# Fused attention and GEGLU on one core: the order of a DMA queue, merged key and query loads, and the end of the kernel

## The chip, the cores and the metric

One core of a Trainium2 chip. The metric is the device time of one execution in microseconds (us), the median of several runs. The program is written with a tile framework: the author gives instructions in program order, and a list scheduler orders each engine's stream by simulated times, unless an engine's order is set by hand.

## The reference

```python
x = A_x                                        # 1 x 2048 x 576, fp32
xn = layernorm(x)                              # no scale, no bias
q, k, v = split(xn @ wqkv)                     # 32 heads of 18
p = softmax(q @ k.T * 18 ** -0.5)
s = (p @ v) @ wo                               # 576 x 576
g = silu((gelu_tanh(xn @ w_gate) * (xn @ w_up)) @ w_down)   # 576 -> 4608 -> 576
out = x + s * g
```

## The kernel before

Everything is fp32 accurate: an operand is cut into a high part (fp32r) and a low part, and a product is three matmuls, high by high, low by high and high by low. The kernel has four stages.

**Prologue.** Layernorm, transposes, the projections. Queries and keys go as high and low parts to `qk` in DRAM, values to `vs`, the normalized x transposed to `xhs`, the cut `wo` to `wos`.

**Sections.** The feed-forward net is 144 sections (`section`): 4 blocks of 512 tokens by 36 tiles of 128 of the 4608 hidden units. A section has 27 pairs of 64-row matmuls (`gate_up`, L421: gate and up at once in the two halves of the array), with work of attention put between them (`spread` over `specials`, and `hooks` before the i-th pair). x of the block stands in six tiles `xd` (high and low, three parts of three 64-row chunks); each is loaded to the lower 64 partitions (`load_xd`, L140, 384 KB) and copied to the upper 64 by `copy_xd` (L146 ScalarE for high, L147 GpSimd for low). The tiles have one buffer, so a new block's parts are loaded in the block's last section, after the 9th, the 18th and the last pair. Weights: `load_gu` (L126, two transfers of 288 KB, two buffers), cut into `wh` and `wl` by `split` on GpSimd (L106, L108). After a section come the activation (`activate`), the sums and cuts for a Strassen-like down projection (`sums_a` L456 to L461, `cut_a` L449, L450 on GpSimd), and after every second section the down products (`downs`, L533, added into `M` by VectorE, L537). Their cut weights `T` (2 MB) are formed in the first pass (`FORMED`), stored (`store_t`, L509) and loaded later (`load_t`, L475).

**Attention inside the sections.** Sections 11 to 138 carry attention: 32 units (8 groups of 4 heads by 4 query blocks), each of 4 sections. A section n has 8 score pairs (L784, exponential on ScalarE L785) of its key chunk and 8 maximum pairs (L749, reduction on VectorE L750), which run 40 slots ahead, and then the products with the values (`values`, L801). Keys are chunks of 512 tokens in 7 buffers of `KA`; a head takes 64 rows of the array: 18 rows high, 18 low, 18 high again (L715 `load_k`, 12 transfers of 36 KB), queries high, high, low (L737), and two rows with the negated maxima, high and low, that are zero (L738, 20 KB of zeros) until the maxima are known. `max_neg` reduces, cuts and transposes the maxima and stores them (L761); `max_end` fetches them, 8 rows by 8 transfers (L772). The lead sections 0 to 10 (`FIRST`) carry only the first unit's maximum pairs.

**Scaling and end.** `load_scale` (L670 `on`, L671 `od`), `scale` (L678), `store_scale` (L687) divide by the sums. The last five sections (`ENDS`) have no attention; between them stand the 16 output tiles: `load_wo` (woh 1.4 MB, wol 1.3 MB), `load_xy` (L916), `split_o`, `gate` (tanh of y on ScalarE L922, then VectorE L923), `project_o` (L933).

All DMAs are issued from SyncE. TensorE runs in program order (`manual_schedule`), the other engines, SyncE among them, in the scheduler's; `tc.keep_in_program_order` holds one instruction behind the one written just before it on its engine.

Of the kernel before, what the change touches and what calls it, by code (L numbers as in the profile page):

```python
# [45 lines left out]
ZR = HR - MROW  # L46
# [31 lines left out]
def kernel(ctx: ExitStack, tc: tile.TileContext, x, wqkv, wo, w_gate, w_up, w_down, out):  # L78
# [15 lines left out]
    mxT = [dram.tile([P, 8 * QD], F32, name=f"mxT{i}") for i in range(2)]  # L94
    ys = dram.tile([S - TB, D], F32, name="ys")
    zeros = dram.tile([P, ZR * TB // P], F32, name="zeros")
# [47 lines left out]
    def copy_xd(x, keep=lambda i: i):  # L144

        keep(nc.scalar.activation(x[0][HR:P], f(x[0])[0:HR], AF.Copy))  # L146
        keep(nc.gpsimd.tensor_copy(x[1][HR:P], x[1][0:HR]))  # L147
# [12 lines left out]
    with tc.tile_pool(name="pro", bufs=1) as pro, tc.tile_pool(name="pps", bufs=1, space=PSUM) as pps:  # L160
# [96 lines left out]
        zz = pro.tile([P, ZR * TB // P], F32, name="zz")  # L257
        nc.gpsimd.memset(zz, 0.0)
        nc.sync.dma_start(zeros, zz)
# [304 lines left out]
    def section(specials=(), tag="f", slots=False):  # L564
# [29 lines left out]
        for p in spread(pairs, specials, 1 if slots else None, hooks):  # L594
            p()
        if nxt:
            split_gu(nxt, NG - 1)
# [96 lines left out]

    with tc.tile_pool(name="att", bufs=1, reuse_waits="tile") as att:
        VS = [att.tile([P, VC * VW + 32 - DH - 1], F32, name=f"VS{i}") for i in range(VB)]
        for i, kk in enumerate(KS):
            for r in range(2):
                (nc.vector, nc.gpsimd)[i % 2].memset(f(kk[r]), 1.0)
        for vv in VS:  # L700
            nc.vector.memset(vv[:, VC * VW:], 0.0)

        def load_k(n, keep=lambda i: i, rs=(0, 1)):
# [4 lines left out]
            cols = slice(c * TB, (c + 1) * TB)  # L708
            for r in rs:
                for a in range(2):  # L710
                    kk = f(KS[n % KB][r])[64 * a:64 * a + MROW, :]
                    h = QD * (u % NQ) + 2 * r + a
                    rows = slice(D + h * DH, D + (h + 1) * DH)
                    for n_, i in enumerate((0, 1, 0)):
                        keep(nc.sync.dma_start(kk[n_ * DH:(n_ + 1) * DH, :], qk[i, rows, cols]))  # L715
# [11 lines left out]
        def load_q(u, rs=(0, 1)):  # L727
            j, g = divmod(u, NQ)
            cols = slice(j * TB, (j + 1) * TB)
            for r in rs:  # L730
                t = QS[u, r] = att.tile([P, TB], F32R, name=f"q{r}", bufs=3)
                for a in range(2):
                    q = f(t)[64 * a:64 * a + MROW, :]
                    h = QD * g + 2 * r + a
                    rows = slice(h * DH, (h + 1) * DH)
                    for n, i in enumerate((0, 0, 1)):
                        nc.sync.dma_start(q[n * DH:(n + 1) * DH, :], qk[i, rows, cols])  # L737
                    nc.sync.dma_start(f(t)[64 * a + MROW:64 * a + HR, :], zeros.rearrange("p c -> (p c)").rearrange("(r t) -> r t", t=TB))  # L738
# [13 lines left out]
        def max_neg(u, keep=lambda i: i):  # L752
# [3 lines left out]
            m2 = att.tile([P, 2, 4 * QD], F32R, name="m2", bufs=2)  # L756
            nc.vector.tensor_copy(m2[:, 0], nm)
            nc.vector.tensor_tensor(m2[:, 1], nm, f(m2)[:, 0], op=ALU.subtract)
            mt = att.tile([P, 8 * QD], F32, name="mt", bufs=2)
            nc.vector.transpose(mt, f(m2).rearrange("p i c -> p (i c)"))  # L760
            nc.sync.dma_start(mxT[u % 2], mt)  # L761
            NM[u] = True

        def max_end(u):

            del NM[u]
            parts = mxT[u % 2].rearrange("(q c) s -> c q s", q=4)
            for a in range(QD):
                for i in range(2):
                    row = 64 * (a % 2) + MROW + i  # L770
                    c = 4 * (i * QD + a)
                    nc.sync.dma_start(f(QS[u, a // 2])[row:row + 1, :].rearrange("o (t q s) -> o t q s", q=4, s=32),  # L772
                                      parts[c:c + 4].rearrange("(o t) q s -> o t q s", o=1))
# [18 lines left out]
        def values(u, kt):  # L792
# [42 lines left out]
        for r in range(2):  # L835
            load_k(0, rs=(r,))
            load_q(0, (r,))
        slot, chunk = 0, 1
        for n, m in enumerate(FIRST):
            none = [lambda: None]  # L840
            lead = [lambda s=s: max_pair(*divmod(s, NS)) for s in range(slot, slot + m)]
            section((n == 2) * 5 * none + lead + (m > 0 and n != 2) * none, "ring" if n == 1 else "f")
            if 0 in NM:
                max_end(0)
            if slot + m >= NS > slot:
                max_neg(0, tc.keep_in_program_order)
            slot += m
            while n > 0 and chunk < KB and chunk * SLOTS <= slot + SLOTS:
                load_k(chunk, tc.keep_in_program_order)
# [7 lines left out]
        ended, scaled = None, 0  # L857
# [168 lines left out]
```

## Time and profile before

| | |
|---|---|
| median of 3 runs | 2645.11 us (2644.92 to 2646.5) |
| the profiled execution, own time | 2650.72 us |
| its span, first to last instruction | 2648.9 us |
| TensorE busy | 2568.8 us, 97% |
| VectorE, GpSimd, ScalarE busy | 2157.7, 1600.7, 1463.6 us |
| mean granted clock of TensorE | 0.988 of full |
| DMA | 445.08 MB, 168 GB/s over the span |

In the views, PE is TensorE, PEld its weight load, DVE VectorE, ACT ScalarE, POOL GpSimd, SPq the queue of SyncE. A row of a timeline gives start, length, engine, line, operation, output<-inputs, a count, and in brackets how long the engine had been idle and what ended that. The rows of SPq are DMA issues; a row's length includes the wait before issues that it merges.

### The profile page before, as it was taken

What the parts mean: (1) busy time and instruction counts of PE and PEld (TensorE: products, weight loads), DVE (VectorE), ACT (ScalarE), POOL (GpSimd) and SP (SyncE); (2) the same over time, 40 slices, a digit from 0 to 9 for tenths busy, and PEclk for the clock granted to TensorE, in tenths of its full rate; (3) what the DMA queues carried; (4) which work ended last, traced back from release to release, by engine and by line L of the source; (5) the groups of instructions that cost most, each with busy time, mean ns of one, the idle gap of its engine ahead of it and who ended that gap; (6) DMA issues with size and microseconds to landing.
All of it is one profiled execution on the core that took longest, in us unless ns stands there. A gap on an engine that the chain in (4) does not pass through costs nothing.

```text
span 2648.9 us, 53876 instructions
## 1 busy us (share of the span) xinstructions
PE 2568.8 (97%) x20548; PEld 1852.7 (70%) x20548; DVE 2157.7 (81%) x2462; ACT 1463.6 (55%) x1741; POOL 1600.7 (60%) x1619
## 2 busy tenths in 40 slices
PE   9999999999989999999989999999998999999978
PEld 8887766666656666666656667666665666667768
DVE  5326899989978998998868888989887898988468
ACT  3222266666657655556556565555555666665622
POOL 2127688778777856666556555656556565555632
PEclk9999999999989999999989999999999999999989
DMA  8875355555565555555565555555565555556583
GB/s 258 261 242 145 86 165 162 166 164 163 160 180 168 168 159 163 164 162 166 164 159 170 165 161 158 162 160 159 158 166 136 159 160 160 160 157 166 163 246 128
DMA packets 393217, 445.08 MB, mean 168 GB/s; under 512 B 116732, under 2 KB 296444, under 8 KB 384384
## 3 DMA queue, kind: packets, MB, share of 16 engines
q1 hardware_dynamic: 392960, 441.64, 57.6%
q8 instruction: 164, 2.69, 0.4%
q14 instruction: 93, 0.76, 0.1%
HBM read 346.22 MB, written 95.28 MB: 167 GB/s over the span
## 4 chain that ended last, share of the span: by engine, by line
PE 75%; POOL 11%; DMA 6%; DVE 4%; issue 2%; ACT 1%; SPq 1%; POOLq 0%; DVEq 0%; ACTq 0%
PE pg L421 18%; PE acc L801 12%; PE py L533 12%; PE pu L421 9%; PE pe L784 7%; PE pm L749 7%; PE po L181 7%; DMA rawd<-in_B_w_down_dram 3%; POOL al L450 2%; POOL wl L108 2%; DMA xd<-xhs 1%; PE py L520 1%; POOL wh L106 1%; POOL T L498 1%; PE po L933 1%
## 5 line engine op out<-in xcount | busy, mean ns | idle before, releaser
L750 DVE TENSOR_REDUCE mx<-pm 128x2 f32<-128x1024 f32 x1024 | 1219.9, 1225 | 208.3 <-PE pm L749 200.9
L785 ACT ACTIVATE pT<-pe 128x1024 f32<-128x1024 f32 x1024 | 1047.6, 1026 | 615.3 <-PE pe L784 577.0
L421 PE MATMUL pu<-xd,wh 64*128 64x512 f32 x2538 | 933.8, 399 | 14.5 <-POOL xd L147 11.0
L421 PE MATMUL pg<-xd,wh 64*128 64x512 f32 x2538 | 932.8, 399 | 13.0 <-DMA xd<-xhs 7.8
L421 PEld LDWEIGHTS pg<-xd,wh 64*128 64x128 f32 x2538 | 471.7, 186 | 129.4 <-issue 61.5
L106 POOL TENSOR_SCALAR wh<-raw 128x384 fp32r<-128x384 f32 x432 | 236.3, 549 | 516.3 <-DMA raw<-in_B_w_up_dram 256.4
L421 PEld LDWEIGHTS pu<-xd,wh 64*128 64x128 f32 x2538 | 471.6, 186 | 41.4 <-POOL xd L147 14.1
L421 PE MATMUL pg<-xd,wl 64*128 64x512 f32 x1269 | 499.8, 394 | 0.0
L421 PE MATMUL pu<-xd,wl 64*128 64x512 f32 x1269 | 499.1, 393 | 0.0
L801 PE MATMUL acc<-pT,VS 128*32 128x512 f32 x4096 | 466.4, 596 | 0.0
L108 POOL TENSOR_TENSOR wl<-raw,wh 128x384 fp32r<-128x384 f32 x432 | 444.4, 1031 | 31.7
L784 PE MATMUL pe<-q,KA 64*128 64x512 f32 x2048 | 420.4, 397 | 14.2 <-DVE mx L750 7.2
L749 PE MATMUL pm<-KA,q 64*128 64x512 f32 x2048 | 422.4, 395 | 3.2 <-ACT pT L785 2.8
L533 PE MATMUL py<-T,ah 128*128 128x288 f32 x1876 | 384.4, 300 | 20.8 <-DVE M L537 17.1
L537 DVE TENSOR_TENSOR M<-py,M 128x576 f32<-128x576 f32 x448 | 337.7, 757 | 30.0 <-PE py L533 16.7
L533 PEld LDWEIGHTS py<-T,ah 128*128 128x128 f32 x1876 | 300.6, 189 | 76.7 <-issue 54.0
L801 PEld LDWEIGHTS acc<-pT,VS 128*32 128x32 f32 x4096 | 120.1, 109 | 277.5 <-issue 231.3
L450 POOL TENSOR_TENSOR al<-h,ah 128x512 fp32r<-128x512 f32 (+1 forms) x139 | 286.5, 2061 | 34.0 <-ACT ah L447 23.7
L784 PEld LDWEIGHTS pe<-q,KA 64*128 64x128 f32 x2048 | 196.5, 185 | 133.6 <-DVE mx L750 39.8
L533 PE MATMUL py<-T,al 128*128 128x288 f32 x938 | 277.4, 296 | 0.6 <-POOL al L450 0.6
L421 PEld LDWEIGHTS pg<-xd,wl 64*128 64x128 f32 x1269 | 236.3, 186 | 31.7
L421 PEld LDWEIGHTS pu<-xd,wl 64*128 64x128 f32 x1269 | 236.3, 186 | 12.3
(152 smaller groups left out, 2906.9 us busy)
## 6 DMA issues: line engine op xcount, KB each, us to landing
T<-ts SPq DMA_DIRECT2D x49, 2016.0 KB
KA<-qk SPq DMA_DIRECT2D x1536, 36.0 KB
raw<-in_B_w_gate_dram SPq DMA_DIRECT2D x144, 288.0 KB
raw<-in_B_w_up_dram SPq DMA_DIRECT2D x144, 288.0 KB
ts<-T SPq DMA_DIRECT2D x18, 2016.0 KB
VS<-vs SPq DMA_DIRECT2D x128, 152.0 KB
qk<-t SPq DMA_DIRECT2D x72, 256.0 KB
q<-qk SPq DMA_DIRECT2D x384, 36.0 KB
```

What stands on the lines that cost most here:

```text
L106: first = nc.gpsimd.tensor_scalar(hi, raw, 1.0, 1.0, op0=ALU.mult, op1=ALU.mult)
L108: keep(nc.gpsimd.tensor_tensor(lo, raw, f(hi), op=ALU.subtract))
L181: nc.tensor.matmul(o, st, m, start=(i == 0), stop=(i == len(terms) - 1))
L421: nc.tensor.matmul(o, w[1 + wp][k][rr, c, :], xd[k][xp][rr, c, :], start=(i == 0), stop=(i == len(terms) - 1))
L450: keep(two.tensor_tensor(lo, raw, f(hi), op=ALU.subtract))
L533: nc.tensor.matmul(py[:, t, 0:DC], h[:, i, tt], T[:, w, k], start=n == 0, stop=n == 2)
L537: nc.vector.tensor_tensor(M[:, m], py[:, :, 0:DC], M[:, m], op=ALU.add)
L749: nc.tensor.matmul(pm[:, a], QS[u, r][rr, t * P:(t + 1) * P], KS[(u * NA + c) % KB][r][rr, :], start=True, stop=True)
L750: nc.vector.tensor_reduce(MX[u][:, 2 * r:2 * r + 2, t, c], pm, axis=AX.X, op=ALU.max)
L784: nc.tensor.matmul(pe[:, a], KS[(u * NA + c) % KB][r][rr, t * P:(t + 1) * P], QS[u, r][rr, :], start=True, stop=True)
L785: nc.scalar.activation(PT[u, kt][:, 2 * r:2 * r + 2, :], pe, AF.Exp, scale=SCALE)
L801: nc.tensor.matmul(ACC[u][32 * a:32 * a + 32, :], VS[(u * NA + c) % VB][:, v:v + 32], pt[:, a, :], start=first, stop=last, skip_group_chec ...
```

## The change

- Both halves (r = 0, 1) of keys and of queries come by one transfer: 6 for a key chunk, 6 + 2 for queries, whose three tiles `QT` are now fixed and zeroed once; only the two rows of the maxima are zeroed again.
- The maxima are laid out so that 4 transfers store them and 2 fetch them; the fetch is at pair 10 of the next section.
- From the attention stage on, SyncE issues in program order. Some loads and stores are written at other places: `load_k` behind its section, the store of the outputs behind the values, `store_scale` one section later.
- `copy_xd` of the second and third part goes in three pieces each.
- In the lead sections ScalarE cuts the high part of the weights; the last three specials of every second one stand behind its pairs.
- At the end x and y of the first tile are loaded ahead of `wo`, the first gate comes behind section 1 of the end and not behind section 0, and an output's store is issued one tile later.

The diff, cut:

```diff
-def spread(pairs, specials, first=None, hooks={}):
+def spread(pairs, specials, first=None, hooks={}, tail=0):
+    specials, ends = specials[:len(specials) - tail], specials[len(specials) - tail:]
...
-    return out
+    return out + list(ends)

-    mxT = [dram.tile([P, 8 * QD], F32, name=f"mxT{i}") for i in range(2)]
+    mxT = [dram.tile([8 * QD, P], F32, name=f"mxT{i}") for i in range(2)]

-    def copy_xd(x, keep=lambda i: i):
-        keep(nc.scalar.activation(x[0][HR:P], f(x[0])[0:HR], AF.Copy))
-        keep(nc.gpsimd.tensor_copy(x[1][HR:P], x[1][0:HR]))
+    def copy_xd(x, keep=lambda i: i, i=slice(None)):
+        keep(nc.scalar.activation(x[0][HR:P, i], f(x[0])[0:HR, i], AF.Copy))
+        keep(nc.gpsimd.tensor_copy(x[1][HR:P, i], x[1][0:HR, i]))

     # section
+        one = split_ap if n + 1 < ATT.start else split
...
-                split_gu(nxt, k)
+                split_gu(nxt, k, one)
...
-                FF["hooks"].setdefault(8 * k - 7, []).append(lambda k=k: copy_xd(xd[k], keep))
+                for i in range(XG):
+                    FF["hooks"].setdefault(8 * k - 7 + 3 * i, []).append(lambda k=k, i=i: copy_xd(xd[k], keep, i))

+    ctx.enter_context(tc.manual_schedule(engines={mybir.EngineType.SP}))
...
+        QT = [att.tile([P, 2, TB], F32R, name=f"QT{i}") for i in range(3)]
+        for t in QT:
+            nc.gpsimd.memset(f(t), 0.0)

-            for r in rs:
-                for a in range(2):
...
-                    for n_, i in enumerate((0, 1, 0)):
-                        keep(nc.sync.dma_start(kk[n_ * DH:(n_ + 1) * DH, :], qk[i, rows, cols]))
+            load_heads(KA[:, i:i + 2], D, u % NQ, c, (0, 1, 0))
+
+        def load_heads(t, row, g, c, parts):
+            rows = slice(row + QD * g * DH, row + QD * (g + 1) * DH)
+            for a in range(2):
+                for m, i in enumerate(parts):
+                    o = HR * a + m * DH
+                    nc.sync.dma_start(f(t)[o:o + DH], qk[i, rows, c * TB:(c + 1) * TB].rearrange("(r a d) t -> a d r t", r=2, a=2)[a])

+        def max_store(u):
+            for q in range(4):
+                qq = slice(32 * q, 32 * q + 32)
+                nc.sync.dma_start(mxT[u % 2][:, qq], NM[u][qq])

     # max_end
+            for a in range(2):
+                o = HR * a + MROW
+                nc.sync.dma_start(f(QT[u % 3])[o:o + 2].rearrange("i r t -> i (r t)"),
+                                  mxT[u % 2][16 * a:16 * a + 16].rearrange("(i x) q -> i (x q)", i=2))

     # values, reciprocals
-                nc.sync.dma_start(oT[g, :, cols], acc)
+                at(u * NA + NA - 1, 1, nc.sync.dma_start, oT[g, :, cols], acc)
...
-            nc.sync.dma_start(rt.rearrange("a (c s) -> a c s", s=QD * TB // P), den)
+            at((u + 1) * NA + 3, 0, nc.sync.dma_start, rt.rearrange("a (c s) -> a c s", s=QD * TB // P), den)

     # lead sections
-            section((n == 2) * 5 * none + lead + (m > 0 and n != 2) * none, "ring" if n == 1 else "f")
+            section((n == 2) * 5 * none + lead + (m > 0 and n != 2) * none, "ring" if n == 1 else "f",
+                    tail=3 * (m > 0 and n % G == 0))

     # attention sections
-            if n > 0:
-                load_k(n - 1 + KB)
             section([p for s in range(s0, s0 + SLOTS) for p in slot_pairs(s)], slots=True)
+            load_k(n + KB)
...
             load_v(n + 2)
+            tasks(n, 1)
+            if ended:
+                max_store(um - 1)
+                FF["hooks"].setdefault(10, []).append(lambda v=um - 1: max_end(v))
             downs()
...
-                at(n + 1, 2, store_scale, scaled)
+                at(n + 2, 0, store_scale, scaled)

     # end
-                nc.sync.dma_start(out[rows, :], xx)
+                outs.append((out[rows, :], xx))
...
+        load_xy(0, 0)
         load_wo()
-        load_xy(0, 0)
...
         for i in range(ENDS):
             section([], "ring" if i % 2 else "f")
+            if i == 1:
+                ready()
             downs()
             finish()
-            if i == 0:
-                ready()
```

More of the change, by code (lines that the diff above doesn't have):

```diff
@@ L45 @@
 RING = 3
-ZR = HR - MROW
 DC, TH = D // 2, TB // 2
@@ L562, in gates, with section @@
         FF["gates"] = []
-    def section(specials=(), tag="f", slots=False):
+    def section(specials=(), tag="f", slots=False, tail=0):
         n = FF["n"]
@@ L593, in section @@
                 hook(9 * k + 9, lambda k=k: xd.append(load_xd(b + 1, k)))
-        for p in spread(pairs, specials, 1 if slots else None, hooks):
+        for p in spread(pairs, specials, 1 if slots else None, hooks, tail):
             p()
         if nxt:
-            split_gu(nxt, NG - 1)
+            split_gu(nxt, NG - 1, one)
         FF["w"] = nxt
@@ L725, with load_q @@
         QS, MX, ACC, SUM, PT, NM, DEN = {}, {}, {}, {}, {}, {}, {}
-        def load_q(u, rs=(0, 1)):
+        def load_q(u):
             j, g = divmod(u, NQ)
[L729 to L738, printed above, removed]
+            t = QT[u % 3]
+            load_heads(t, 0, g, j, (0, 0, 1))
+            for a in range(2):
+                o = HR * a + MROW
+                nc.sync.dma_start(f(t)[o:o + 2].rearrange("i r t -> i (r t)"), zeros)
+            for r in range(2):
+                QS[u, r] = t[:, r]
         def max_pair(u, i):
@@ L755, in max_neg @@
             keep(nc.vector.tensor_reduce(nm, MX[u].rearrange("p a t c -> p (a t) c"), axis=AX.X, op=ALU.max, negate=True))
-            m2 = att.tile([P, 2, 4 * QD], F32R, name="m2", bufs=2)
-            nc.vector.tensor_copy(m2[:, 0], nm)
-            nc.vector.tensor_tensor(m2[:, 1], nm, f(m2)[:, 0], op=ALU.subtract)
+            m2 = att.tile([P, 2, 2, 2, 4], F32R, name="m2", bufs=2)
+            n2 = nm.rearrange("p (r a t) -> p a r t", r=2, a=2)
+            nc.vector.tensor_copy(m2[:, :, 0], n2)
+            nc.vector.tensor_tensor(m2[:, :, 1], n2, f(m2)[:, :, 0], op=ALU.subtract)
             mt = att.tile([P, 8 * QD], F32, name="mt", bufs=2)
-            nc.vector.transpose(mt, f(m2).rearrange("p i c -> p (i c)"))
-            nc.sync.dma_start(mxT[u % 2], mt)
-            NM[u] = True
+            nc.vector.transpose(mt, f(m2).rearrange("p a i r t -> p (a i r t)"))
+            NM[u] = mt
+        def max_store(u):
+            for q in range(4):
+                qq = slice(32 * q, 32 * q + 32)
+                nc.sync.dma_start(mxT[u % 2][:, qq], NM[u][qq])
         def max_end(u):
             del NM[u]
[L767 to L773, printed above, removed]
+            for a in range(2):
+                o = HR * a + MROW
+                nc.sync.dma_start(f(QT[u % 3])[o:o + 2].rearrange("i r t -> i (r t)"),
+                                  mxT[u % 2][16 * a:16 * a + 16].rearrange("(i x) q -> i (x q)", i=2))
         def score_pair(u, i):
@@ L856 @@
             finish()
-        ended, scaled = None, 0
+        scaled = 0
         for n in range(NU * NA):
```

48 lines of the change are left out of this document (22 added, 26 removed).

## The prediction

> **What bounds the kernel now.** I read the page first, then busy time by stretch, then the timelines of single engines in the stretches that lose time.
>
> ```profile
> span 2648.9 us, 53876 instructions
> ...
> PE 2568.8 (97%) x20548; PEld 1852.7 (70%) x20548; DVE 2157.7 (81%) x2462; ACT 1463.6 (55%) x1741; POOL 1600.7 (60%) x1619
> ```
>
> TensorE sets the time: outside 80 us it is busy. So a change pays only where TensorE waits, or where it runs at a lowered clock after a wait. The second view is busy time by stretch: stretch and its length, then PE, PEld, DVE, ACT and POOL busy with their instructions, granted clock, DMA share, GB/s.
>
> ```profile
> 1226.24:1259.48 33.24, 33.24 (x283) 23.07 (x286) 28.89 (x31) 20.31 (x24) 20.13 (x21) 1.00 0.59 170
> 1329.56:1343.32 13.76, 13.76 (x119) 8.94 (x119) 12.26 (x13) 9.83 (x11) 9.86 (x9) 1.00 0.59 144
> 742.06:768.48 26.42, 20.70 (x120) 12.57 (x119) 11.54 (x11) 14.85 (x15) 21.48 (x20) 0.74 0.70 157
> 1362.76:1390.73 27.97, 18.05 (x123) 11.03 (x119) 11.47 (x11) 14.75 (x15) 15.63 (x15) 0.76 0.78 167
> 1983.24:2008.18 24.94, 17.50 (x119) 10.23 (x119) 11.62 (x11) 14.27 (x15) 17.75 (x17) 0.93 0.59 127
> 2513.35:2541.70 28.35, 10.19 (x86) 8.22 (x85) 10.57 (x16) 4.98 (x7) 6.48 (x10) 0.79 0.99 281
> 2541.70:2546.88 5.18, 5.18 (x21) 5.18 (x22) 3.82 (x6) 0.00 (x0) 2.95 (x3) 0.50 0.82 187
> ...
> 235.50:335.00 99.50, 93.63 (x717) 78.44 (x719) 81.36 (x90) 29.18 (x42) 63.42 (x66) 0.97 0.43 114
> ```
>
> Row 1 is a pair of sections in the attention loop: 33.24 of 33.24 us, nothing to win. Row 2 is one section with its values: 13.76 us. Rows 3 to 5 are the same work right after a change of token block: 12.66, 14.21 and 11.18 us more. Call them B1, B2, B3. Row 6 holds a hole at the end, where the DMA engines are full (share 0.99, 281 GB/s). The last row, the lead sections, has 5.87 us idle. B1 to B3 and the end hole are therefore the prize.
>
> **The block changes.** A new block's x is six transfers xd (384 KB each), copied to the upper partitions by ScalarE (high parts) and GpSimd (low parts). SyncE's queue at B2, B3 and B1:
>
> ```profile
> 1349.11 0.33 SPq L475 DMA_DIRECT2D T<-ts  x1
> ...
> 1350.82 11.28 SPq L715 DMA_DIRECT2D KA<-qk  x12
> ...
> 1363.65 4.03 SPq L140 DMA_DIRECT2D xd<-xhs  x6
> ...
> 1369.62 0.76 PE L421 MATMUL pg<-xd,wh 64*128 64x512 f32 x1 [6.79 <-DMA xd<-xhs]
> ```
> ```profile
> 1969.52 0.57 SPq L475 DMA_DIRECT2D T<-ts  x1
> ...
> 1972.76 4.47 SPq L140 DMA_DIRECT2D xd<-xhs  x4
> ...
> 1979.32 2.12 SPq L140 DMA_DIRECT2D xd<-xhs  x2
> ```
> ```profile
> 733.47 0.35 SPq L509 DMA_DIRECT2D ts<-T  x1
> 733.87 4.82 SPq L140 DMA_DIRECT2D xd<-xhs  x4
> ...
> 739.44 1.24 SPq L140 DMA_DIRECT2D xd<-xhs  x2
> ```
>
> At B2 the xd loads sit behind twelve key loads that block the queue for 11.28 us. At B1 the 2 MB store of T goes out just ahead of them. At B3 they already leave where the changed program's text puts them: two each after the 9th and 18th of the 27 pairs, the last two at the section's end. So B3 is a picture of B2 after the change, and its other engines show what is late next:
>
> ```profile
> 1982.76 1.48 ACT L146 ACTIVATE xd<-xd 64x1536 fp32r<-64x1536 f32 x1 [0.86 <-DMA xd<-xhs]
> ```
> ```profile
> 1984.77 1.46 POOL L147 CAST xd<-xd 64x1536 fp32r<-64x1536 f32 x1 [2.24 <-DMA xd<-xhs]
> ...
> 1990.13 1.46 POOL L147 CAST xd<-xd 64x1536 fp32r<-64x1536 f32 x1 [2.21 <-DMA xd<-xhs]
> 1991.67 1.28 POOL L459 TENSOR_TENSOR h<-h,h 128x512 f32<-128x512 f32 x1
> ...
> 1998.72 1.46 POOL L147 CAST xd<-xd 64x1536 fp32r<-64x1536 f32 x1
> ```
> ```profile
> 2000.23 0.50 PE L421 MATMUL pu<-xd,wh 64*128 64x512 f32 x1 [3.57 <-POOL xd L147]
> ```
>
> With T's 2 MB ahead the first part lands 10 us after its issue, the next 2.0 us later. Then GpSimd does 7.05 us of sums and cuts (1991.67 to 1998.72) between the second copy and the third, and TensorE waits 3.57 us for the third. Loads that start sooner don't remove that; only the order on GpSimd does, and the list scheduler still sets it.
>
> B3: the loads move by nothing. In pieces, the first third of a copy is done after a third of 1.46, about 0.5 us: TensorE's third part starts 1.0 us sooner. Gain 1.0. B2: B3's picture, plus on and od (0.5 MB, just behind T, estimated 1.3 us at twice B3's rate of 2.0 us per 384 KB, as those two go to 128 partitions and xd to 64). B3 loses 11.18, minus 1.0 for pieces, plus 1.3: 11.5. Gain 14.2 - 11.5 = 2.7. B1: the T store now stands behind xd, keys and values in the program. Its section begins at 742.06 - 13.76 = 728.3, so xd goes at 731.7 (a third of 10.2 us later), with no large transfer ahead. B2's first part took 6 us from 1363.65 to 1369.62, so here 737.7, then one each 2.0 us: the second low part 743.7, the third 747.7. First third copied 744.2, needed 745.8. Pieces to 745.3, then the 7.05 us of sums to 752.3, third part 752.8, needed 749.2: 3.6 us late, with the ScalarE copy about 4. Gain 12.66 - 4 = 8.7. Bounds: if GpSimd takes the copies ahead of its sums at all three, some 7 us more at B2 and B3 and 3 at B1; if it takes the sums ahead of the second copy too, up to 4 less at B1. Block changes: 8.7 + 2.7 + 1.0 = 12.4 (8 to 29). ScalarE's nine pieces cost two more fixed starts per copy, on an engine with 45% free.
>
> **The end.** The rows of SyncE, VectorE and TensorE, and the wait:
>
> ```profile
> 2513.35 0.38 SPq L475 DMA_DIRECT2D T<-ts  x1
> ...
> 2522.40 0.38 SPq L899 DMA_DIRECT2D wol<-wos  x1
> ...
> 2524.00 0.43 SPq L916 DMA_DIRECT2D yy<-ys  x1
> ```
> ```profile
> PE py L533 <- DVE M L537: 16.3, 1, 16.3
> ...
> 2523.63 0.50 PE L533 MATMUL py<-T,ah 128*128 128x288 f32 x2 [1.91 <-DMA T<-ts]
> ...
> 2537.44 0.76 DVE L923 SCALAR_TENSOR_TENSOR th<-th,yy 128x576 f32<-128x576 f32 x1 [14.02 <-ACT th L922]
> ...
> 2548.15 0.30 PE L933 MATMUL po<-woh,oh 128*128 128x288 f32 x1
> ```
>
> VectorE's gate for the first output tile waits for yy, which went out behind all of wo, 1.4 MB of woh and 1.3 MB of wol; the additions into M queue behind the gate, their PSUM buffers stay full, and TensorE stands 16.3 us. After: x and yy go ahead of wo. T stays where it is, 2513.4, and its products begin about 2523.6 as now. Behind it are 0.6 MB of x and yy, so yy is there around 2524, the gate 1.5 us later; products end at 2523.6 + 5.8 + 1.5 = 2530.9. The output product needs woh and wol: 2.0 + 0.6 + 1.4 + 1.3 = 5.3 MB at 281 GB/s from 2514 end at 2533, about 2535 with 2 us to land. So 2548.15 becomes 2535: 13.2. A wait of 4 us is left before it. What it costs in clock is unknown: after the 16.3 us the clock stood at 0.50 for 5.18 us (row 7), which is 2.6 us of work; B3's 3.57 us left its stretch at 0.93. I take 1.2 of 0 to 2.6, so 12 (bounds 3 to 17: 3 if wo comes as late as now, 17 if nothing waits). [...] Outputs stored one group later cost nothing: four x buffers cover them, and without that cover SyncE would hold the next loads for one addition on GpSimd, 2 us.
>
> **Merged transfers and queue order in the loop.**
>
> ```profile
> 1568.91 9.13 SPq L715 DMA_DIRECT2D KA<-qk  x12
> 1578.14 0.68 SPq L126 DMA_DIRECT2D raw<-in_B_w_gate_dram  x1
> ...
> 2037.17 4.28 SPq L715 DMA_DIRECT2D KA<-qk  x12
> ```
> ```profile
> 1583.62 0.98 POOL L106 TENSOR_SCALAR wh<-raw 128x384 fp32r<-128x384 f32 x2 [9.96 <-DMA raw<-in_B_w_up_dram]
> ```
>
> Twelve key loads take 4.28 us to issue when free, six 2.1; queries go from 16 issues to 8, the maxima's rows from 1 + 8 to 4 + 2. All run beside a busy TensorE: worth 0 on the path. If the cover were gone, it would be 2.1 us a section. Order: raw weights now go at a section's top. At 1568.5 that is 9.6 us sooner than the 1578.14 shown; every other one waits for the values' end (the next at 1582.5, against 1586 now), since the V load waits there for TensorE, and T, outputs and raw queue behind it. Key chunk n+7 leaves at the end of section n and is read in section n+2, 13.76 us later. The store of the maxima waits for VectorE's transpose; behind it stand the raw loads, and who waits is GpSimd, two sections ahead of need. So 0, with rival 3 as the bound above. Three more memsets of queries fall on GpSimd before the first section.
>
> **The lead.**
>
> ```profile
> 188.56 0.66 SPq L126 DMA_DIRECT2D raw<-in_B_w_gate_dram  x1
> ```
> ```profile
> 189.65 4.27 DVE L699 MEMSET KA<- 128x512 f32 x8
> ```
> ```profile
> 204.98 0.39 PE L421 MATMUL pgu<-xd,wh 64*128 64x512 f32 x2
> ```
>
> The weights of section 1 went out at 188.56. In program order they stand behind 14 key and query loads, which wait for the memset at 189.65: 190.2 + 14 x 0.36 = 195.2, cut by about 202 (5.5 us lie between the issue at 1578.14 and the cut at 1583.62), needed at 204.98. No loss; if the query buffers come free only at 199, it is 5 to 8 us. Against that, ScalarE's share of the cuts can win at most the 5.87 us idle of the lead. Three maxima at the tail of five sections each set up to one reduction (1.2 us) ahead of the down products. I take 0 (-6 to +8).
>
> **Sum.** 12.4 + 12 = 24.4. The profiled span 2648.9 becomes 2624.5; the profiled run's own time, 2650.72, about 2626; the median, 2645.11, about 2620.5. A difference of 0.2% (5.3 us) is about what a measurement tells from none.
>
> **Rivals.**
> 1. The new queue order makes the scheduler put the copies ahead of GpSimd's sums. For it: smaller pieces leave openings. Against: in all three traces' stretches that I read, the sums came before the third copy. Gains 11.7 + 9.7 + 8 + 12 = 41: 2604.
> 2. The end hole only changes its cause, T and wo on full DMA engines instead of yy: for it, share 0.99; against, 16 us is more than 5.3 MB need. Gains 12.4 + 3: 2630.
> 3. Slower: in strict order the raw loads wait behind the V load and land too late for GpSimd's cuts, each pair of sections. The loop has 64 pairs; it decides from 24.4 / 64 = 0.38 us a pair. At 0.7 us it costs 45: 2665. For it: GpSimd already waits up to 9.96 us for raw. Against: the cut is then two sections ahead of use, and raw goes out earlier, not later.
> 4. It doesn't do what it says: the other engines are re-sorted around the same waits, a new VectorE gate stands in front of M, and nothing is left: 2643.
>
> **How the numbers follow.** Forecast 0.45, rival 1 0.25, rival 2 0.12, rival 3 0.12, rival 4 0.06. The range runs from 2598 (rival 1 with some lead gain) to 2642 (rival 2 with the lead's 8 us and B1's 4), and leaves out rival 3 and most of rival 4. Faster: 0.45 + 0.25 + 0.12 + 0.01; same: 0.05 of rival 4; slower: rival 3.
>
> **What would show it.** Right: the stretch after B1 is near 18 us, B2 25, B3 24; the six xd loads leave before any key load; TensorE's 16.3 us wait for M is gone and one of some 4 us for wol stands before the first output product; row 1's pair stays 33.2 us. Wrong: pairs of sections longer than 33.2 us, a TensorE wait for wh or KA in the loop, GpSimd's third copy ahead of its sums, or the first section 1 matmul later than 205.

## The result and the profile after

The changed kernel takes 2673.3 us (median of 4 runs, 2670.96 to 2675.37) against 2645.02 (2641.91 to 2646.5) before: ratio 1.0108, interval [1.0091, 1.0126]. It is slower by 28 us; 2620.5 was forecast. The page, first lines, and the stretches that answer to those of the prediction (start and end, length, then PE, PEld, DVE, ACT, POOL busy, granted clock, DMA share, GB/s): B1, B2, B3, the pair and the lead.

```profile
span 2670.2 us, 52622 instructions
...
PE 2573.9 (96%) x20548; PEld 1850.8 (69%) x20548; DVE 2146.0 (80%) x2462; ACT 1476.0 (55%) x1783; POOL 1585.5 (59%) x1604
```
```profile
762.44:779.60 17.16, 15.80 (x124) 9.26 (x121) 11.80 (x12) 14.28 (x19) 12.89 (x15) 1.00 0.91 259
1374.93:1406.62 31.69, 18.95 (x119) 11.81 (x120) 11.78 (x12) 15.45 (x19) 17.79 (x20) 0.73 0.57 119
1996.34:2018.74 22.40, 18.03 (x120) 11.28 (x120) 11.73 (x12) 15.56 (x19) 16.22 (x18) 0.85 0.67 145
1237.94:1271.12 33.18, 33.18 (x283) 23.15 (x279) 29.01 (x31) 20.30 (x24) 20.13 (x21) 1.00 0.60 168
243.88:350.03 106.15, 93.87 (x719) 77.93 (x715) 77.25 (x90) 37.24 (x60) 55.20 (x50) 0.95 0.34 85
```

B1 (17.16 us) and B3 (22.40) came out about as forecast (18, 24), the pair is unchanged, B2 (31.69, forecast 25) is worse than before, and the lead is 7 us longer. Where the time went is read best from TensorE's progress. All traces hold the same 20,548 matmuls, nearly in the same order, so the starts of number 1000, 2000, 2200, 5400, 5900, 10350, 10700, 15400, 15800, 19600 and 20000 cut each run into the same pieces of work, from the first matmul's start to the last one's. First column: us of before; then the difference to it for the changed kernel and for five of the experiments below.

| piece | before | change | e1 | e4 | e9 | e12 | e13 |
|---|---|---|---|---|---|---|---|
| prologue | 187.0 | -1.4 | -1.1 | +0.1 | -0.3 | -1.2 | -0.7 |
| lead | 136.7 | +10.4 | +3.1 | +3.2 | +1.6 | +4.8 | -1.1 |
| loop's start | 24.5 | +6.1 | -0.1 | -0.1 | -0.2 | -0.1 | 0.0 |
| first block | 387.2 | +5.4 | +7.5 | +5.6 | +5.0 | -1.7 | -1.3 |
| around B1 | 78.5 | -10.5 | -3.3 | -9.4 | -9.4 | -10.6 | -9.4 |
| second block | 536.1 | +2.2 | +1.5 | +2.0 | +2.5 | +0.7 | +1.2 |
| around B2 | 60.4 | +3.1 | +1.3 | +4.9 | -8.4 | -8.7 | -8.4 |
| third block | 565.3 | -2.1 | +0.1 | -0.6 | -1.6 | -1.4 | -0.9 |
| around B3 | 64.4 | -2.0 | +3.2 | -2.7 | -7.1 | -9.1 | -9.0 |
| fourth block | 455.0 | +1.0 | +2.1 | -0.1 | +0.3 | +2.9 | +0.2 |
| end, first part | 70.8 | -4.4 | +3.7 | -2.5 | -2.3 | -4.2 | -2.0 |
| end, second part | 73.8 | +13.4 | 0.0 | +2.4 | +0.7 | +1.8 | +1.9 |

The profiled run of before (2650.72 us) lies 5.7 above its median, and the changed kernel's (2671.98) 1.3 below its own, so the change's column sums to 21 where the medians differ by 28; the other columns are too low by some 4 to 8 in the same way. Single pieces of unchanged work wander by 1 to 3 us from run to run.

**The lead.** TensorE's waits in 200 to 350 us (total, times, longest), then SyncE's queue:

```profile
PE pgu L421 <- ACT wh L112: 6.1, 1, 6.1
PE pm L756 <- ACT pT L794: 5.1, 1, 5.1
PE py L520 <- DVE mx L757: 3.1, 5, 0.6
```
```profile
184.85 13.39 SPq L305 DMA_DIRECT2D vs<-vn  x8
198.34 2.12 SPq L724 DMA_DIRECT2D KA<-qk  x6
...
203.69 0.66 SPq L126 DMA_DIRECT2D raw<-in_B_w_gate_dram  x1
```

Section 1's weights leave at 203.69, not at 188.56: in program order they stand behind eight value stores, which wait up to 1.5 us each, 10.8 us together, for ScalarE to write their tiles. TensorE stops for 6.1 us and comes back at a granted clock of 0.53:

```profile
203.79:209.90 6.11, 0.00 (x0) 0.00 (x0) 1.98 (x3) 4.20 (x7) 1.26 (x1) 0.83 0.92 215
209.90:214.90 5.00, 4.71 (x22) 3.41 (x24) 0.00 (x0) 2.91 (x6) 4.78 (x5) 0.53 0.63 158
```

The second wait, 5.1 us, starts at SyncE too (its own waits, 290 to 340 us): the store of the first maxima waits 21 us for VectorE's transpose at the head of the queue, the next raw weights behind it leave at 324.43 instead of 305.57, GpSimd cuts and sums late (it waits 8.86 us for raw and begins at 331.64), and ScalarE's cut of T, which waits 7.77 us for the sums and begins at 337.52, stands ahead of the exponentials pT (339.50).

```profile
SPq L774 <- DVE mt L768: 21.0, 1, 21.0
```

Nothing leaves SyncE for those 21.0 us: the issue before them ends at 298.92, the next one begins at 319.99.

**The first block.** TensorE's waits for pT (total, times, longest), one every four sections, and SyncE, GpSimd and ScalarE around one of them:

```profile
PE pm L756 <- ACT pT L794: 5.0, 5, 1.8
```
```profile
456.05 1.71 SPq L774 DMA_DIRECT2D mxT<-mt  x4
457.85 0.37 SPq L509 DMA_DIRECT2D ts<-T  x1
458.32 0.60 SPq L126 DMA_DIRECT2D raw<-in_B_w_gate_dram  x1
```
```profile
469.93 0.51 POOL L106 TENSOR_SCALAR wh<-raw 128x384 fp32r<-128x384 f32 x1 [6.82 <-DMA raw<-in_B_w_up_dram]
```
```profile
475.94 1.17 ACT L490 ACTIVATE T<-tsum 128x1152 fp32r<-128x1152 f32 x1 [8.07 <-POOL tsum L483]
...
477.92 1.92 ACT L794 ACTIVATE pT<-pe 128x1024 f32<-128x1024 f32 x2
```

**B2.** SyncE, TensorE's waits, and GpSimd:

```profile
1361.24 0.33 SPq L475 DMA_DIRECT2D T<-ts  x1
1361.74 0.32 SPq L672 DMA_DIRECT2D on<-oT  x1
1362.11 0.56 SPq L673 DMA_DIRECT2D od<-rT  x1
1362.71 0.67 SPq L126 DMA_DIRECT2D raw<-in_B_w_gate_dram  x1
1363.43 3.63 SPq L126 DMA_DIRECT2D raw<-in_B_w_up_dram  x1
1367.16 8.64 SPq L140 DMA_DIRECT2D xd<-xhs  x6
```
```profile
PE pg L421 <- DMA xd<-xhs: 6.0, 1, 6.0
PE pu L421 <- POOL xd L147: 5.7, 1, 5.7
```
```profile
1375.32 1.26 POOL L680 TENSOR_TENSOR on<-on,od 128x512 f32<-128x512 f32 x1 [8.96 <-DMA od<-rT]
...
1379.96 1.26 POOL L459 TENSOR_TENSOR h<-h,h 128x512 f32<-128x512 f32 x1
...
1388.64 3.14 POOL L147 CAST xd<-xd 64x1536 fp32r<-64x1536 f32 x4
```

T, on, od and raw, 3.1 MB, go ahead of xd; its first part lands about 13.7 us after its issue (1367.16 to 1380.84, where ScalarE's copy begins). GpSimd, too, stands 8.96 us for od, which is behind T, so its sums and cuts start late and its copies of xd, the first one among them, come behind them at 1388.64.

**The end.** SyncE, VectorE, TensorE's waits from 2515 us on, and SyncE's own wait for stored outputs in the changed kernel (2550 to 2660 us) and, for the same stage, before (2535 to 2640 us):

```profile
2530.56 0.56 SPq L837 DMA_DIRECT2D rT<-rec  x1
2531.21 0.39 SPq L475 DMA_DIRECT2D T<-ts  x1
2532.33 0.34 SPq L925 DMA_DIRECT2D xx<-in_A_x_dram  x1
2532.73 0.59 SPq L925 DMA_DIRECT2D yy<-ys  x1
```
```profile
2542.91 0.76 DVE L932 SCALAR_TENSOR_TENSOR th<-th,yy 128x576 f32<-128x576 f32 x1 [6.52 <-ACT th L931]
...
2548.29 0.75 DVE L537 TENSOR_TENSOR M<-py,M 128x576 f32<-128x576 f32 x1
```
```profile
PE py L533 <- DVE M L537: 8.5, 5, 6.6
PE po L942 <- DVE ol L917: 7.7, 2, 5.7
```
```profile
SPq L925 <- DMA out_dram<-xx: 38.4, 11, 8.6
```
```profile
SPq L916 <- DMA out_dram<-xx: 7.5, 5, 2.1
```

In program order T goes behind the store of the last reciprocals, which waits 13.6 us for VectorE, and yy behind T. The gate still stands ahead of the additions into M. The second wait is new: an output product waits 5.7 us for a cut that stands on VectorE behind the next gate, whose yy came late. It came late because the load of x ahead of it on SyncE waits until an earlier output, in the same buffer, has landed in DRAM: 11 times, 38.4 us in all, against 7.5 us before.

### The profile page after: what moved, and what is told of

Same layout as the page of the kernel before. It is cut to its first block, busy times and chain, and to the rows that moved or that the text cites. A ratio compares the mean times of both kernels' runs of the same rounds, so it can differ in the third digit from the quotient of the medians.

```text
span 2670.2 us, 52622 instructions
## 1 busy us (share of the span) xinstructions
PE 2573.9 (96%) x20548; PEld 1850.8 (69%) x20548; DVE 2146.0 (80%) x2462; ACT 1476.0 (55%) x1783; POOL 1585.5 (59%) x1604
## 5 line engine op out<-in xcount | busy, mean ns | idle before, releaser
L106 POOL TENSOR_SCALAR wh<-raw 128x384 fp32r<-128x384 f32 x402 | 218.1, 547 | 448.2 <-DMA raw<-in_B_w_up_dram 234.3
L756 PE MATMUL pm<-KA,QT 64*128 64x512 f32 x2048 | 417.8, 396 | 16.3 <-ACT pT L794 15.4
L108 POOL TENSOR_TENSOR wl<-raw,wh 128x384 fp32r<-128x384 f32 x402 | 415.5, 1038 | 26.0
L793 PE MATMUL pe<-QT,KA 64*128 64x512 f32 x2048 | 418.3, 397 | 12.8 <-DVE mx L757 8.2
L793 PEld LDWEIGHTS pe<-QT,KA 64*128 64x128 f32 x2048 | 196.4, 185 | 130.1 <-DVE mx L757 29.3
L756 PEld LDWEIGHTS pm<-KA,QT 64*128 64x128 f32 x2048 | 202.5, 186 | 66.5 <-ACT pT L794 24.7
```

Of the source, the lines that this page charges most:

```text
L106: first = nc.gpsimd.tensor_scalar(hi, raw, 1.0, 1.0, op0=ALU.mult, op1=ALU.mult)
L108: keep(nc.gpsimd.tensor_tensor(lo, raw, f(hi), op=ALU.subtract))
L756: nc.tensor.matmul(pm[:, a], QS[u, r][rr, t * P:(t + 1) * P], KS[(u * NA + c) % KB][r][rr, :], start=True, stop=True)
L793: nc.tensor.matmul(pe[:, a], KS[(u * NA + c) % KB][r][rr, t * P:(t + 1) * P], QS[u, r][rr, :], start=True, stop=True)
```

## The experiments

All ran beside the kernel before. Theory S: the strict order on SyncE loses the time, where an issue that waits stands ahead of a load that TensorE needs soon. Rival R: the change's other parts lose it.

**e1: no strict order.**
```diff
-    ctx.enter_context(tc.manual_schedule(engines={mybir.EngineType.SP}))
```


> The changed kernel without the line that puts SyncE's issues in program order; all its other parts stay. Theory S (strict order on SyncE is what loses): the lead loses 15 us less (no 6.1 us wait for the first cut weights of section 1, no 5.1 us wait at the loop's start) and the end about 9 less, while the block changes may lose their 10 us of gain again, because the 2 MB store of T may stand ahead of xd again: 2640 to 2658 us, the first section 1 matmul near 205 us. Theory R (the other parts lose: ScalarE's share of the weight cuts, three maxima at the tail of a lead section, the first gate later): the time stays within 5 us of 2673.

2667.14 us (1.0082 [1.0066, 1.0098]): outside both forecasts. The table shows why the sum moves by only 6: the order costs 13.5 in the lead and loop's start and 13.4 in the end's second part, and it earns 7 at B1, 5 at B3 and 8 in the end's first part. The first block loses with and without it; without it TensorE's waits there are others (3.8 us for VectorE's sums `accs`, none for pT), so the other parts cost something there too.

**e2: that line alone, on the kernel before.**
```diff
+    ctx.enter_context(tc.manual_schedule(engines={mybir.EngineType.SP}))
     with tc.tile_pool(name="att", bufs=1, reuse_waits="tile") as att:
```


> The kernel before, with that one line alone added at the same place. Theory S: the lead's raw weights wait behind the value stores and the key and query loads, here 28 issues instead of 14, so the lead loses 15 us or more; with the end 2660 to 2680 us. Theory R: within 5 us of 2645.

2782.85 us (1.0518 [1.0502, 1.0533]), far over what S expected. The first block alone is 78 us longer, and its waits (340 to 830 us, TensorE's and SyncE's own) are those of the changed kernel tenfold:

```profile
PE pm L751 <- ACT pT L787: 48.7, 12, 4.8
```
```profile
SPq L724 <- PE acc L803: 80.9, 6, 14.5
SPq L763 <- DVE mt L762: 79.6, 6, 14.2
```

The value load and the maxima's store wait at the head of the queue and raw waits behind them. So what else the change does, the places that it gives them in the program above all, makes the order bearable; no run separates the places from the merged transfers.

**e3, e4: strict order from the attention loop on; and in the loop alone.**
```diff
         scaled = 0
+        strict = ExitStack()
+        strict.enter_context(tc.manual_schedule(engines={mybir.EngineType.SP}))
         for n in range(NU * NA):
...
+        strict.close()        # e4 only
```


> The changed kernel with the strict order beginning only at the attention loop, so that the lead sections are list-scheduled on SyncE. Theory S: the lead's 15 us come back and nothing else moves: 2658 (2655 to 2662). Theory R: the lead's loss stays, 2673.

> As the one before, and the strict order also ends after the attention loop, so that the end sections and the output products are list-scheduled on SyncE. Theory S: the lead's 15 us and the end's 9 come back, the block changes keep their 10 and the end may gain some of what was forecast: 2635 to 2649. Theory R: 2673.

2664.57 (1.0069 [1.0052, 1.0086]) and 2652.31 (1.0020 [1.0008, 1.0032]). Both lie above what S expected (2655 to 2662, 2635 to 2649). The difference between them, 12.3 us, is nearly all the end's second part (+13.6 and +2.4): S holds there. In the lead and the loop's start the order is worth 7.2 + 6.2 us; some 3 stay.

**e5: the changed kernel, two issues moved in the lead.**
```diff
+                if b == NB - 1 and j in (0, 1):      # among the value stores
+                    early[j + 1] = load_gu(j + 1, tc.keep_in_program_order)
...
-                max_store(0)
+                FF["hooks"].setdefault(3, []).append(lambda: max_store(0))
```


> The changed kernel, strict order and all, with two issues moved in the program: the raw weights of sections 1 and 2 among the value stores of the last token block, and the store of the first maxima to the fourth pair of the next section, behind that section's raw loads. Theory S (what waits at the head of SyncE's queue is what loses, in the lead the value stores and the maxima's store): the waits of 6.1 us (203.8) and 5.1 us (335.5) go, the lead is some 7 and the loop's start 6 us shorter: 2658 to 2662 us. Rival R (ScalarE's cuts and the maxima at a section's tail lose the lead): less than 3 us of change, 2670 to 2675.

2667.31 (1.0095 [1.0079, 1.0111]), between the two forecasts. The 6.1 us wait is gone, and the loop's start waits 2.1 us instead of 5.1, as S says. The lead gives back only 2 of its 10: new waits for `wl` (3.4 us in all) come in, as GpSimd has the same cuts to do.

**e6: the changed kernel, T ahead of the store of the last reciprocals.**
```diff
             downs()
-            tasks(n, 2)
+            if n < NU * NA - 1:
+                tasks(n, 2)
             finish()
+            if n == NU * NA - 1:
+                tasks(n, 2)
```


> The changed kernel with the last T load ahead of the store of the last reciprocals in program order, nothing else. Theory S: T goes out when its buffer is free (about 2525 instead of 2531), the 8.4 us of wait at 2539 to 2549 shrink to some 3: 5 us less at the end's first part, 2667 to 2669; the waits for yy at 2586 stay. Rival (DMA engines full at the end, the cause only changes): the hole keeps its length, 2672 to 2674.

2676.57 (1.0125 [1.0110, 1.0140]), above both forecasts: S's step failed, and the hole changed its cause, as the rival says. T left at 2526.4 and its wait went. But xx and yy left only at 2534.5: SyncE waited 7.0 us until the 8 KB store of the reciprocals, issued just behind T's 2 MB, had landed. TensorE waited 7.5 us for M instead of 6.6.

**e7, e9: e4 with T behind xd at B2 and B3.** In e7 the load of the very last T was missing, so its end is not read; e9 has it.
```diff
-            if g == 0:
+            if g == 0 and (n + 2) % (NR * G) == 0 and n + 2 < NF:   # e7: without n + 2 < NF
+                FF["late_t"] = r
+            elif g == 0:
                 load_t(r)
...
             xd.append(load_xd(b + 1, NG - 1))
+            if "late_t" in FF:
+                load_t(FF.pop("late_t"))
```


> The kernel whose strict order covers the attention loop alone (2652), with the load of T moved behind the six xd loads at the second and third change of token block. Theory: T's 2 MB ahead of xd are what keeps xd late there, and T has some 20 us to spare; the wait of 6.0 us for the first part at the second change goes, that at the third (2.8 us) too, and part of the waits for copies: 6 to 12 us less, 2640 to 2646. Rival (GpSimd's sums and cuts set the third part anyway): at most 3 us less, 2649 to 2652.

> The changed kernel with SyncE's program order in the attention loop alone and T loaded behind the six xd loads at the second and third change of block (the load of T for the very last section stays where it was). Theory: the second and third change lose some 12 and 6 us less than with T ahead, as in the run before, and the end is that of the loop-only kernel: 2652 - 18 = 2634 (2630 to 2640). Rival: the earlier run was short because its end lacked the last T: 2640 to 2646.

e7 2635.5 (0.9968 [0.9956, 0.9981]), better than its forecast; e9 2634.13 (0.9954 [0.9938, 0.9970]), as forecast, so its rival falls. In e9 B2 gains 13.3 on e4, B3 4.4. B2 and B3 of e9, by stretch:

```profile
1362.05:1381.52 19.47, 16.53 (x120) 10.71 (x121) 11.90 (x13) 14.29 (x19) 12.48 (x14) 0.91 0.75 217
1972.51:1989.85 17.34, 15.79 (x120) 9.39 (x120) 11.79 (x12) 14.31 (x19) 12.49 (x14) 1.00 0.83 240
```

**e8: the merged transfers alone, on the kernel before** (its own order; `load_k`, `load_q`, `max_neg`, `max_end` and the tiles of the change).

> The kernel before with the merged transfers alone (six key loads and eight query transfers, maxima's rows by four stores and two loads, their tile's layout), at the places and in the free order of before. Theory M (the merged transfers and what the list scheduler makes of them cost the 5 to 7 us of the first token block's sections that every variant shows): the first block's stretch is 5 us longer, 2650 or more. Rival (they cost nothing; it is the order of the program's text): 2643 to 2647.

2661.26 (1.0074 [1.0056, 1.0091]): they cost 17 us by the medians, spread over all blocks (3.5, 4.0, 1.5, 2.5 us) without one wait that carries it. The price that the prediction put at nothing is real in free order; its cause is not shown.

**e10: e9 without two parts of the change in the lead.**
```diff
-        one = split_ap if n + 1 < ATT.start else split
+        one = split
...
-            section(..., tail=3 * (m > 0 and n % G == 0))
+            section(...)
```


> As the one before, with two parts of the change undone in the lead: GpSimd alone cuts the weights, and no maxima stand at a section's tail. Theory P (those two parts, not the order, hold the 3 us that the lead still loses): the lead is 3 us shorter, 2631 if the one before is 2634. Rival: 0, or slower, since GpSimd's cuts were late.

2625.76 (0.9927 [0.9908, 0.9945]): 8.4 us less than e9, and the lead is 5.8 us shorter. Theory P holds, with about twice the size.

**e11: e9 with whole copies.**
```diff
-                for i in range(XG):
-                    FF["hooks"].setdefault(8 * k - 7 + 3 * i, []).append(lambda k=k, i=i: copy_xd(xd[k], keep, i))
+                FF["hooks"].setdefault(8 * k - 7, []).append(lambda k=k: copy_xd(xd[k], keep))
```


> As the first of this call, with the second and third copy of xd whole again. By the prediction's own step a third part can start some 1.0 us sooner with pieces: 1 us lost at each of three changes, 3 us, 2637 if the first is 2634. Rival (pieces also let ScalarE's and GpSimd's queues serve TensorE in between, about 3 us a change): 2643. Rival (nothing, the order of the sums decides): 2634.

2634.19 (0.9954 [0.9939, 0.9968]) against 2634.13: the pieces are worth nothing that can be measured.

**e12: e9 with the maxima stored later.**
```diff
-                max_store(um - 1)
+                FF["hooks"].setdefault(3, []).append(lambda v=um - 1: max_store(v))
```


> As the first of this call, with the store of the maxima at the fourth pair of the next section, behind that section's raw loads. Theory Q (a small form of the prediction's third rival: in the first block the store waits for VectorE's transpose at the head of the queue, raw comes late, GpSimd's cuts and sums come late, ScalarE's cut of T waits for them and holds pT, five waits of 0.6 to 1.7 us): those waits go, the first block is 4 to 5 us shorter, 2630 if the first is 2634. Rival: the waits stay.

2623.84 (0.9919 [0.9902, 0.9936]): 10 us less than e9, where 4 were forecast. The first block is 6.7 us shorter, and TensorE hardly waits there:

```profile
335.00:730.00 395.00, 394.23 (x3285) 271.13 (x3283) 356.06 (x390) 260.21 (x301) 321.61 (x309) 1.00 0.56 164
```

Theory Q's chain holds, but not its first link: in e9 the store waits only 0.6 us a time for the transpose. More of what was moved out of raw's way is the 1.71 us that the four stores take to issue.

**e13: e10 and e12 together; e14: the end's edits undone; e15: one transfer for each head; e16: the tail kept.**
```diff
 # e14
+        load_wo()
         load_xy(0, 0)
-        load_wo()
...
-                outs.append((out[rows, :], xx))
+                nc.sync.dma_start(out[rows, :], xx)
...
-            if i == 1:
-                ready()
             downs()
             finish()
+            if i == 0:
+                ready()
 # e15
-                    nc.sync.dma_start(f(t)[o:o + DH], qk[...].rearrange("(r a d) t -> a d r t", r=2, a=2)[a])
+                    for r in range(2):
+                        nc.sync.dma_start(f(t)[o:o + DH, r], qk[...].rearrange("(r a d) t -> a d r t", r=2, a=2)[a, :, r])
```


> The edits of the two best runs together: strict order in the loop alone, T behind xd, the maxima's store behind the next raw loads, the lead without ScalarE's cuts and without a tail. If the two gains add (8.4 for the lead, 10.3 for the store of the maxima, both against 2634): 2615.5. If the lead's gain and the first block's are the same wait: 2624.

> As the first, with the end's edits undone: wo ahead of the first x and yy, the first gate after the first end section, outputs stored at once. By the prediction's step they are worth 12 us: 2627 if the first is 2615. Its second rival (T, wo, x and yy on full DMA engines, the hole only changes its cause): 0 to 3 us, 2615 to 2618.

> As the first, with one key or query transfer for each head again (12 and 12 issues of 36 KB instead of 6 and 6 of 72 KB). Theory A (the merged transfers themselves are slower on the chip): up to 15 us faster, 2600 to 2610. Theory B (merging cost only what the free list scheduler made of it; in program order the queue is short either way): 2614 to 2618. Theory C (in strict order every issue counts, and the longer queue makes raw late): slower, 2620 or more.

> As the first, with the three maxima at the tail of a lead section kept, and GpSimd still cutting alone. If the tail holds the lead's loss (TensorE waits 0.6 us for a reduction ahead of the down products, five times, and the last three pairs have nothing beside them): 2618 to 2621. If ScalarE's cuts hold it: 2615.5, the lead as short as in the first.

e13: 2619.28 us (0.9893 [0.9877, 0.9910]), the fastest, 1.1% under the kernel before; it lies between the two forecasts, so the gains add in part. e14: 2621.31 (0.9907 [0.9892, 0.9922]): the end's edits are worth about 2 us, not 12, and the two intervals overlap. Its hole and e13's (2480 to 2520 us), e13 first:

```profile
PE py L533 <- DMA T<-ts: 6.9, 1, 6.9
PE py L533 <- DVE M L537: 5.2, 1, 5.2
```
```profile
PE py L533 <- DVE M L537: 9.4, 1, 9.4
PE py L533 <- DMA T<-ts: 5.2, 1, 5.2
```

The wait for M is 4.2 shorter and that for T 1.7 longer. e15: 2630.9 (0.9941 [0.9926, 0.9956]): theory C. The loss is at B1 and B2 (5.4 and 8.3 us); at B2 the key loads ahead of xd take 5.50 us to issue instead of 2.10, and TensorE waits 5.2 us for xd's first part, which it didn't in e13. Merging the key and query loads thus earns 12 us in program order. The 17 us of e8 are for more than that, the maxima's transfers and the fixed query tiles too, so the two runs don't price the same edit in two orders. e16: 2621.64 (0.9910 [0.9894, 0.9925]), not to be told from e13 by its time. Here TensorE's gaps tell more, which are steadier than the pieces (with the same gaps the lead took 138.3 us in e9 at a granted clock of 1.00, and 141.5 in e12 at 0.98): in the lead they sum to 6.6 us in e10, e13 and e14, to 10.1 in e16, and to 11.2 in e4, e9, e11 and e12, which have the tail and ScalarE's cuts. So the tail idles TensorE for 3.5 us (five waits of 0.6 us for a reduction are 3.1 of it) and ScalarE's cuts for 1.1.

**e17: e13 with T first, as in e6; e18: e17 with the gate behind the down products.**
```diff
             downs()
             finish()
+            if i == 1:                 # e18: moved down from ahead of downs()
+                ready()
```


> The fastest variant so far (2619.3) with the last load of T ahead of the store of the last reciprocals in the program. Theory: T leaves when its buffer is free (about 2484.5 instead of 2494.3), TensorE's 6.9 us wait for T goes; x and yy still come 2 us after 2494 and the wait for M takes over part of it: the end's first part 3 to 7 us shorter, 2612 to 2616. Rival (the hole only changes its cause): within 2 us of 2619.

> As the one before, with the first gate behind the down products and the sums of the second end section instead of ahead of them, so that no addition into M stands behind the wait for yy. Theory: the wait for M (5.2 us) goes as well, what is left is a wait of at most 4 us for wo or yy before the first output product: 2606 to 2612. Rival (the output product waits for yy or wo as long): as the one before.

2631.42 (0.9953 [0.9938, 0.9968]) and 2630.95 (0.9953 [0.9937, 0.9970]), 12 us slower than e13: both misses. In e17 T left at 2493.56, hardly sooner than in e13 (2494.32): both stand behind a read of the last output that leaves only when the store of it, issued at 2484.13, has landed. The rows of SyncE, and its own wait (2490 to 2510 us):

```profile
2484.13 0.44 SPq L661 DMA_DIRECT2D oT<-accs  x1
2493.14 0.33 SPq L676 DMA_DIRECT2D on<-oT  x1
2493.56 0.83 SPq L475 DMA_DIRECT2D T<-ts  x1
...
2503.30 0.34 SPq L932 DMA_DIRECT2D xx<-in_A_x_dram  x1
```
```profile
SPq L932 <- DMA rT<-rec: 7.6, 1, 7.6
```

Then xx waited until 2503.30, as in e6: its load needs the store of the reciprocals landed, and that store, 8 KB, now went out behind T's 2 MB. In e13, with the store ahead of T, this wait is 1.3 us. TensorE's waits for M grew to 16.4 us. How short the end can be stays open.

## Why the prediction was wrong, step by step

- **B1** (gain 8.7): the size is right, 26.42 became 17.16, and e1 shows the cause named, the queue's order: without it the stretch around B1 gains 3.3 instead of 10.5. But what is left is not what was forecast. No wait of 4 us for the third copy appears; TensorE waits 1.1 us in the stretch, for pT, and the rest is a slower pace of its matmuls (15.80 us busy where row 2 has 13.76, both at full clock), which no run explains. That the remainder has the forecast size is luck.
- **B2** (gain 2.7): wrong, 3.7 longer. The step that failed is "So B3 is a picture of B2 after the change". The 1.3 us for on and od are an estimate at twice xd's rate, and no run prices the two alone; the trace of before moves 400 GB/s at a DMA share of 0.94 behind the issues of T, on and od (1353 to 1356) and 215 at 1.10 behind those of xd (1978 to 1983). "Plus on and od" left out raw, 0.6 MB more ahead of xd, whose second issue took 3.63 us, and it left out GpSimd, which waited 8.96 us for od and so did its sums ahead of all copies: TensorE's wait for a copy by GpSimd grew from 2.1 to 5.7 us. It also took T's place ahead of xd as given; with T behind, B2 takes 19.47 us (e9). How much each of these costs is not separated.
- **B3** (gain 1.0): 2.5, right in sign, by luck: the gain was to come from the pieces. **Pieces** (1.0 each): worth nothing (e11); in the changed kernel a piece takes 0.61 us on GpSimd and 0.63 on ScalarE, a whole copy 1.46 and 1.48. Rival 1 did not occur: GpSimd's sums came ahead of the third copy at all three changes, ahead of the second too at B3, and of all at B2.
- **The end** (gain 12): two steps failed. "T stays where it is, 2513.4": T went behind the last reciprocals. Even in free order the edits gain about 2 (e14): rival 2, the hole only changes its cause, is what happened, and its 3 us was about the right size. The argument against it, "16 us is more than 5.3 MB need", goes against the prediction's own sum, in which 5.3 MB take 19 us, without the 2 us to land (an estimate; the first load of the trace of before, 288 KB issued at 0.73, is read at 3.64). And "Outputs stored one group later cost nothing: four x buffers cover them" failed in strict order: loads of x waited 38.4 us for stored outputs to land, and the end's second part, which comes out 13.4 longer, has 13.6 with and 2.4 without the strict order (e3, e4). The bound "3 to 17" held no loss. No run has the strict order with the outputs stored at once.
- **The loop** (0): right for the pair (33.18), wrong for the first block (+5.4). Rival 3's mechanism is real, raw late behind a queue, but once every four sections of one block, 1.0 us each, not at all 64 pairs. "The store of the maxima ... who waits is GpSimd, two sections ahead of need" is the sentence that failed: e12 shows the need.
- **The lead** (0, -6 to +8): the largest miss, 16.5 with the loop's start. "In program order they stand behind 14 key and query loads" left out the eight value stores, 13.39 us of queue, and its own sign, the first matmul of section 1 later than 205, came (209.90); the maxima's store, 21 us, was not priced there. ScalarE's cuts and the tail, costed at "at most win 5.87" and "up to 1.2 each", idle TensorE for 1.1 and 3.5 us (e16), and both together cost 5.8 us of the lead (e10 against e9).
- **The clock.** After the 6.11 us wait TensorE ran 5.00 us at 0.53, which loses 2.35 us of work, after the 5.7 us wait before an output product 5.00 us at 0.52 (2592.33 to 2597.33), which loses 2.4, and after the 16.3 us wait of before 5.18 us at 0.50, which loses 2.6. The 1.2 us taken for a wait of 4 us at the end was a choice between 0 and 2.6.

The sum by the table: block changes -9.4 (forecast -12.4), end +9.0 (-12), lead and loop's start +16.5 (0), first block +5.4 (0), the rest -0.3: 21.2 us of span.

## What to carry to other kernels

An engine's queue in program order is a new resource: for each stretch, write down every issue that stands ahead of each load in the new order, those that the old order had let pass too, and ask which of them waits for a compute engine. Put stores and anything that waits behind the next loads (but ahead of a large transfer, if a next load needs the store landed), large loads with time to spare behind the small urgent ones, and hold the order only where the text was written for it. Cut two traces at the same matmul numbers before explaining anything: a sum of +21 hid pieces from -10 to +13.

## What the runs showed that was not expected

- Four small stores ahead of the weights, 1.71 us of issue and 0.6 us of wait, were enough to stall TensorE through SyncE's queue, GpSimd and ScalarE, once every four sections (e12: 6.7 us over the first block).
- The merged transfers cost 17 us under the list scheduler (e8), and those of keys and queries earn 12 in program order (e15).
- An 8 KB store issued behind a load of 2 MB held up the next load on SyncE, which needed it landed, for 7.6 us; issued ahead of it, for 1.3 us (e17, e13).
- A read of a tensor just stored left SyncE 9.0 us after the store's issue (2484.13 to 2493.14) and held the whole queue.
